# Attention and SwiGLU on one core: an earlier weight load, down weights split between copies, and bank readings moved behind a phase's last copies

## The chip, the core and the metric

The kernel runs on one core of a Trainium2 chip. Its engines work side by side, each through its own list of instructions in order: TensorE (PE, matmuls; PEld is its weight load), VectorE (DVE), ScalarE (ACT), GpSimd (POOL) and SyncE (SP), which issues most of the DMAs. The metric is the device time of one execution in microseconds (us), as the median of several runs; less is better. One execution is also profiled, and times inside it count from its first instruction.

## What is computed

```python
xn = layernorm(x)                        # x: 2048 x 512, fp32
q, k, v = heads(xn @ wqkv)               # 32 heads of 16
s = softmax(q @ k.T * 16 ** -0.5) @ v    # full attention, no mask
s = merge(s) @ wo
g = silu((silu(xn @ w_gate) * (xn @ w_up)) @ w_down)    # hidden width 1792
out = x + s * g
```

All products are made in fp32 precision: an operand is split into a rounded part (hi) and a remainder (lo), and three matmuls (hi hi, lo hi, hi lo) stand for one.

## The kernel before

**A prologue** (up to about 160 us of the span) makes layernorm, the projections q, k and v, and stores them to DRAM. It also makes the first gate and up tile of the FFN. Its last DMA is the store of the last value rows (`made()`, line 835). The buffers of the main part (`att`, lines 839 to 849: `kst`, `vst`, `hh`, `wd`) lie in memory that the prologue used.

**The main part** runs attention and the FFN as one interleaved stream. Attention has 32 units (8 groups of 4 heads by 4 query tiles of 512), each over 16 key tiles. The stream is cut into 101 **blocks** (line 464 on) of 3 to 6 key tiles, numbered from 0 in what follows. In each block, TensorE first runs a list of events, and then `values` (line 375) multiplies the block's probabilities with v into the bank `acc[0]`; `x32`, `x40` and `x48` matmuls of line 379 are the values of 4, 5 and 6 key tiles.

The events of a block come from `events` (line 483), which writes the order out by formula:

- **F**: one step of the other work (FFN, then the output projection): two matmuls that run side by side, one into each of the banks `bankx` and `banky` (`both`, line 184). `fill` (line 442) takes the next step from a generator: `ffn(b)` (line 195), then `project_out` (line 342).
- **D**: the scores of one pair of heads, straight into a PSUM buffer, from which ScalarE takes the exponential (line 889).
- **A, B**: the scores of a pair, one half each, into the one spare bank (`acc[1]`). VectorE copies each half to SBUF (lines 901 and 907), and ScalarE takes the exponential later, from the copy (line 913). B can't start until the copy of A has left the bank, and the next A waits for the copy of B.

How many pairs of a block go by A and B is `copied` (line 487): the smaller of `need` and `fit` (line 486).

**The FFN's order.** A gate and up tile (7 in a group, two groups for each of 4 token tiles) is one phase of 24 steps, then follow four down phases of 21 steps (line 234), one for each 128 tokens. One phase goes into one block. `load_gu` (line 121) loads gate and up weights for the tile after the next, 512 KB into one of two `gur` buffers, and `split_gu` splits them for the next tile; `split_wd` (line 151) splits one tile of down weights. Splits are **chores**: VectorE work in a list with a cost in step lengths. The loop of a block (line 909) puts a chore out when the VectorE has room before its next copy; `tidy` (line 139) puts out all that are left at once. `tidy` is called ahead of a block's last F (line 880), at a block's end (line 914), and in the first step of a group's first down phase (line 233), right behind `split_wd` of the group's last tile (line 230).

**Bank readings.** Behind the last step of a down phase, VectorE reads both banks (lines 241 and 242, or 245 and 246), and the output projection does the same (lines 353 and 354, or 359 and 360). They are put out in the same step as the last matmul.

**Ends.** When a unit is through, `finish` (line 407) adds chores in the unit after it: transpose `acc[0]` (line 390), a reciprocal (395), a multiplication (399), and in every second group a second transpose (415), at the end of the kernel also a split (425, 429). They go to the list at the second D.

Of the kernel before, what the change touches and what calls it, by code (L numbers as in the profile page):

```python
# [9 lines left out]
F32 = mybir.dt.float32  # L10
# [4 lines left out]
ALU = mybir.AluOpType  # L15
# [4 lines left out]
P = 128  # L20
S = 2048
D = 512
# [3 lines left out]
NB = 4  # L26
TB = S // NB
NT = TB // P
# [3 lines left out]
NF = F // P  # L32
# [18 lines left out]
def tile_block(ctx: ExitStack, tc: tile.TileContext, x, wqkv, wo, w_gate, w_up, w_down, out):  # L51
# [15 lines left out]
    one = ctx.enter_context(tc.tile_pool(name="one", bufs=1))  # L67
# [71 lines left out]
    def tidy(room=None):  # L139
        while chores and (room is None or chores[0][0] <= room):  # L140
            cost, work = chores.pop(0)
            work()  # L142
            if room is not None:
                room -= cost
# [19 lines left out]
    def catch_up():  # L164
        while after:
            after.pop(0)()
# [25 lines left out]
        pool.dma_start(g_d[r:r + P], y)  # L192


    def ffn(b):
        for grp, part in enumerate(GROUPS):
            nf = part.stop - part.start
            for f in range(nf):
                i = b * NF + part.start + f
                if i + 1 < NB * NF:  # L200
                    split_gu(i + 1)
                if f:
                    split_wd(f - 1, i - 1)
                    chores.append((0, partial(load_wd, i)))
                elif i:
                    load_wd(i)
                if i + 2 < NB * NF:
                    load_gu(i + 2)
                hi, lo = gu.pop(i)
                n = 0  # L210
                for c in range(DC):
                    for wt, j in ((hi, 0), (hi, 1), (lo, 0)):
                        both(wt[:, c], fx[:, j, c], n == 0, n == 3 * DC - 1)
                        n += 1
                        if n == 3 * DC:
                            th = one.tile([P, TB], F32, tag="th", name="th")
                            ga = two.tile([P, TB], F32, tag="ga", name="ga")
                            act(th, bankx, AF.Tanh, scale=0.5)  # L218
                            dve.scalar_tensor_tensor(ga, th, 1.0, bankx, op0=ALU.add, op1=ALU.mult)  # L219
                            dve.scalar_tensor_tensor(ga, ga, 0.5, banky, op0=ALU.mult, op1=ALU.mult)  # L220
                            kept.append((f, ga))
                            if now == 0:
                                kept.insert(0, first_hidden)
                            if now >= 0:
                                split_hidden()
                            if grp == 1 and f == nf - 1 and b + 1 < NB:
                                load_fx(b + 1, 0)
                                load_fx(b + 1, 1)
                        yield 3 * DC - n
            split_wd(nf - 1, b * NF + part.stop - 1)  # L230
            if grp == 1 and b == NB - 1:
                chores.append((0, partial(load_wo, 0)))
            tidy()
            for t in range(NT):
                n = 0
                for f in range(nf):
                    for a, w in ((0, 0), (0, 1), (1, 0)):
                        both(hh[:, f, a, t * P:(t + 1) * P], wd[:, f, w], n == 0, n == 3 * nf - 1)
                        n += 1
                        if n == 3 * nf and grp == 0:  # L240
                            dve.tensor_copy(facc[:, t], bankx)
                            dve.tensor_add(facc[:, t], banky, facc[:, t])
                        elif n == 3 * nf:
                            y = two.tile([P, D], F32, tag="ga", name="y")
                            dve.tensor_add(y, bankx, facc[:, t])
                            dve.tensor_add(y, banky, y)
                            after.append(partial(store_gate, y, b * TB + t * P))
                            if b == NB - 1:
                                after.append(partial(next_out, t))
                        yield 3 * nf - n  # L250


# [84 lines left out]
    def store_out(t, y):  # L337
        pool.tensor_mul(y, y, gt[t % NT])
        pool.tensor_add(xr[t], y, xr[t])
        (pool if t < end - 1 else sp).dma_start(out[rows[t]], xr[t])  # L340

    def project_out(b, n=DT):
        catch_up()
        for j in range(NT if n == DT else EARLY):
            t = b * NT + j
            i = 0
            for c in range(n):
                for a, w in ((0, 0), (0, 1), (1, 0)):
                    both(lhs[b, c][a][:, j * P:(j + 1) * P], fx[:, w, c], i == 0, i == 3 * n - 1)
                    i += 1  # L350
                    if i == 3 * n and n == DT:
                        y = one.tile([P, D], F32, tag="th", name="y")
                        dve.tensor_scalar(y, bankx, 0.5, None, op0=ALU.mult)
                        dve.scalar_tensor_tensor(y, banky, 0.5, y, op0=ALU.mult, op1=ALU.add)
                        store_out(t, y)
                        if b + 2 < NB:
                            after.append(partial(load_gates, t + NT))
                    elif i == 3 * n:
                        dve.tensor_copy(facc[:, j], bankx)
                        dve.tensor_add(facc[:, j], banky, facc[:, j])  # L360
                    yield 3 * n - i

    def load_gate():
# [119 lines left out]
    def events(n, f):  # L483
        length = 2 * n + f
        need = 2 * n - max(2, (10 * length + 46) // 40)
        fit = 1 if ends and length < 24 else (10 * length + 34) // 112
        copied = max(0, min(need, fit)) if now else 0
        direct = 2 * n - copied
        gap = max(4, min(5, (length - 8) / max(1, direct - 2)))
        marks = [(0, "D"), (1, "D")] + [(7 + gap * i, "D") for i in range(direct - 2)]  # L490
        marks += [(2.2 + max(5.6, min(8, (length - 5) / (2 * copied))) * i, "AB"[i % 2]) for i in range(2 * copied)]
        marks.sort(key=lambda mark: mark[0] - 0.6 * (mark[1] == "D"))
        out = []
        at = left = 0
        for t, kind in marks:
            while left < f - (kind != "D") and at < t:
                out.append((at, "F"))
                left += 1
                at += 1
            out.append((at, kind))  # L500
            at += 1 if kind == "D" else 0.5
        return direct, out + [(at + i, "F") for i in range(f - left)]
# [340 lines left out]
    wd = att.tile([P, FG, 2, D], F32R, name="wd")  # L843
    score = [spool.tile([P, 2, 512], F32, name=f"score{i}") for i in range(2)]
    spare_bank = acc[1]
    ring(2, RING, att)
    queries(1, att)
    load_k(0, 2)
# [8 lines left out]
    def run(u, first, n):  # L857
# [19 lines left out]
        final = max(at for at, (_, e) in enumerate(todo) if e == "F")  # L877
        free = 0
        for at, (t, e) in enumerate(todo):
            if at == final:  # L880
                tidy()
            if e == "F":
                fill(1)
            elif e == "D":
                kt, j = straight[done]
                for h in order():
                    scores(score[done % 2][:, h], kt, j, h)
                probs[kt, j] = ppool.tile([P, 2, TB], F32, tag="pr", name="pr")
                act(probs[kt, j], score[done % 2], AF.Exp, scale=0.25)  # L889
                done += 1  # L890
                if done == 2:
                    while ends:
                        ends.pop(0)()
                    out_steps()
            elif e == "A":
                kt, j = copies.pop(0)
                waiting.append((kt, j))
                scores(spare_bank, kt, j, 0)
                lower = True
                probs[kt, j] = ppool.tile([P, 2, TB], F32, tag="pr", name="pr")  # L900
                dve.tensor_copy(probs[kt, j][:, 0], spare_bank)  # L901
                free = copying.pop(0) + 3
            else:
                kt, j = waiting[-1]
                scores(spare_bank, kt, j, 1)
                lower = False
                dve.tensor_copy(probs[kt, j][:, 1], spare_bank)  # L907
                free = copying.pop(0) + 3
            while chores and at < final and (not copying or max(free, t) + chores[0][0] <= copying[0] + 0.5):
                free = max(free, t) + chores[0][0]  # L910
                chores.pop(0)[1]()
# [28 lines left out]
            ends.append(partial(finish, u))  # L940

    fill(total)
    catch_up()
    assert not queue and not after and given == total
    hi = two.tile([P, 2, D], F32R, tag="guh", name="rh")[:, 0]
# [75 lines left out]
```

## Time and profile before

| | us |
|---|---|
| median of 3 runs | 1419.13 (1418.51 to 1419.31) |
| the profiled execution | 1417.5 |
| its span, first to last instruction | 1415.7 |
| TensorE busy | 1399.6 (99%) |
| ScalarE busy | 1081.4 (76%) |
| VectorE busy | 756.9 (53%) |
| GpSimd busy | 92.0 (7%) |
| mean granted TensorE clock | 0.999 |

A busy TensorE is not one at its peak: matmuls are pipelined, so the time between two starts matters, not the duration of one. A row of the timeline has the start, the length, the engine, the line, the operation, its tiles and how many were merged; in square brackets stand the idle time of the engine just before it, and who ended that. A row of the chain has start, length and what ran.

### The profile page before, as it was taken

How to read it: one execution, taken by the hardware profiler on the slowest of the kernel's cores; microseconds unless marked ns; L12 is line 12 of the kernel's file. 1: busy time of each engine (PE TensorE's matmuls, PEld its weight loads, DVE VectorE, ACT ScalarE, POOL GpSimd, SP SyncE). 2: the span in 40 equal slices, each digit the busy share in tenths (PEclk: the TensorE clock that was granted, in tenths of full speed). 3: DMA queues.
4: the chain of work that ended last, by engine and by line, in shares of the span. 5: the costliest groups of instructions: out<-in, count | busy, mean ns of one | idle time of the engine just before them, and what ended most of it. 6: DMA issues, size and time to landing. Idle time of an engine off the chain costs nothing.

```text
span 1415.7 us, 27730 instructions
## 1 busy us (share of the span) xinstructions
PE 1399.6 (99%) x11227; PEld 853.3 (60%) x11227; DVE 756.9 (53%) x1281; ACT 1081.4 (76%) x1235; POOL 92.0 (7%) x104
## 2 busy tenths in 40 slices
PE   9999999999999999999999999999999999999998
PEld 7777665566555655565566556655565565565555
DVE  6543455346545653555456545654565346556566
ACT  6733587787788777887887788778877787787885
POOL 4200200000000000000000000000000000000333
PEclk9999999999999999999999999999999999999999
DMA  7768642034543421144524403256224123234332
GB/s 220 262 243 255 168 111 57 13 87 93 116 108 106 116 62 35 47 120 101 123 67 105 103 13 72 73 145 148 63 67 114 31 46 72 68 92 137 118 110 101
DMA packets 126956, 148.17 MB, mean 105 GB/s; under 512 B 12524, under 2 KB 79340, under 8 KB 126052
## 3 DMA queue, kind: packets, MB, share of 16 engines
q1 hardware_dynamic: 121620, 125.79, 34.8%
q0 software_dynamic: 4912, 20.12, 3.8%
q8 instruction: 91, 1.49, 0.5%
q14 instruction: 45, 0.37, 0.1%
q10 hardware_dynamic: 288, 0.39, 0.1%
HBM read 106.68 MB, written 39.58 MB: 103 GB/s over the span
## 4 chain that ended last, share of the span: by engine, by line
PE 86%; DVE 1%; ACT 1%; issue 0%; DVEq 0%; ACTq 0%
PE acc L379 32%; PE bankx L186 24%; PE score L873 16%; PE banky L186 11%; PE acc L873 3%; ACT pr L889 1%; PE acc L958 0%; DVE wd L142 0%; PE banky L958 0%; DVE o L390 0%; DVE pr L901 0%; PE score L958 0%; DVE o L415 0%; DVE on L399 0%; DVE rl L395 0%
## 5 line engine op out<-in xcount | busy, mean ns | idle before, releaser
L889 ACT ACTIVATE pr<-score 128x1024 f32<-128x1024 f32 x861 | 813.8, 1033 | 241.3 <-PE score L873 240.1
L379 PE MATMUL acc<-pr,vst 128*17 128x512 f32 x4096 | 463.7, 593 | 0.0
L873 PE MATMUL score<-qst,kst 50*128 50x512 f32 x1722 | 395.1, 414 | 1.7 <-ACT pr L889 1.7
L186 PE MATMUL bankx<-fx,guh 64*128 64x512 f32 x896 | 334.0, 393 | 0.1
L186 PE MATMUL banky<-fx,guh 64*128 64x512 f32 x896 | 325.4, 393 | 0.0
L379 PEld LDWEIGHTS acc<-pr,vst 128*17 128x17 f32 x4096 | 111.2, 97 | 293.2 <-issue 266.6
L873 PEld LDWEIGHTS score<-qst,kst 50*128 50x128 f32 x1722 | 174.6, 184 | 150.4 <-issue 75.7
L901 DVE COPY pr<-acc 128x512 f32<-128x512 f32 x163 | 112.7, 691 | 185.2 <-PE acc L873 180.0
L186 PE MATMUL bankx<-wd,hh 64*128 64x512 f32 x672 | 200.1, 392 | 0.0
L186 PE MATMUL banky<-wd,hh 64*128 64x512 f32 x672 | 197.4, 392 | 0.0
L186 PEld LDWEIGHTS bankx<-fx,guh 64*128 64x128 f32 x896 | 166.9, 186 | 18.8 <-issue 0.9
L186 PE MATMUL banky<-fx,gul 64*128 64x512 f32 x448 | 175.8, 392 | 0.0
L186 PE MATMUL bankx<-fx,gul 64*128 64x512 f32 x448 | 175.8, 392 | 0.0
L186 PEld LDWEIGHTS banky<-fx,guh 64*128 64x128 f32 x896 | 166.8, 186 | 6.1
L913 ACT ACTIVATE pr<-pr 128x1024 f32<-128x1024 f32 x163 | 167.7, 1080 | 0.0
L907 DVE COPY pr<-acc 128x512 f32<-128x512 f32 x163 | 112.6, 691 | 78.2 <-PE acc L873 69.0
L873 PE MATMUL acc<-qst,kst 50*128 50x512 f32 x326 | 131.5, 403 | 6.7 <-DVE pr L901 3.8
L219 DVE SCALAR_TENSOR_TENSOR ga<-th,bankx 128x512 f32<-128x512 f32 x56 | 38.5, 687 | 179.2 <-ACT th L218 179.2
L186 PEld LDWEIGHTS bankx<-wd,hh 64*128 64x128 f32 x672 | 124.9, 186 | 11.9
L186 PEld LDWEIGHTS banky<-wd,hh 64*128 64x128 f32 x672 | 124.5, 186 | 4.2
L186 PEld LDWEIGHTS bankx<-fx,gul 64*128 64x128 f32 x448 | 83.9, 187 | 11.0
L186 PEld LDWEIGHTS banky<-fx,gul 64*128 64x128 f32 x448 | 83.7, 187 | 2.8
(169 smaller groups left out, 1315.5 us busy)
## 6 DMA issues: line engine op xcount, KB each, us to landing
gur<-in_B_w_gate_dram SPq DMA_DIRECT2D x56, 256.0 KB
gur<-in_B_w_up_dram SPq DMA_DIRECT2D x56, 256.0 KB
wdr<-in_B_w_down_dram SPq DMA_DIRECT2D x56, 256.0 KB
kst<-k_d SPq DMA_DIRECT2D x192, 64.0 KB
qst<-q_d SPq DMA_DIRECT2D x192, 64.0 KB
fx<-xt_d SPq DMA_DIRECT2D x24, 512.0 KB
q_d<-parts SPq DMA_DIRECT2D x16, 512.0 KB
k_d<-parts SPq DMA_DIRECT2D x16, 512.0 KB
```

Source lines behind the costliest of these rows:

```text
L186: mm(banks[i], lhs[halves[i]], rhs[halves[i]], start=start, stop=stop)
L219: dve.scalar_tensor_tensor(ga, th, 1.0, bankx, op0=ALU.add, op1=ALU.mult)
L379: mm(acc[0][h * 32:h * 32 + DH + 1], v[:, kt % CT, h * (DH + 1):(h + 1) * (DH + 1)], probs[kt, h // 2][:, h % 2], start=kt == 0, stop=kt = ...
L873: mm(bank, k[r, j, kc * P:(kc + 1) * P], q[r, j], start=True, stop=True)
L889: act(probs[kt, j], score[done % 2], AF.Exp, scale=0.25)
L901: dve.tensor_copy(probs[kt, j][:, 0], spare_bank)
L907: dve.tensor_copy(probs[kt, j][:, 1], spare_bank)
L913: act(probs[kt, j], probs[kt, j], AF.Exp, scale=0.25)
```

## The change

There are four edits.

1. `load_gu(3)` stands ahead of `ring(2, ...)`, behind the prologue; the same load is left out at its place in tile 1 of the FFN.
2. In a group's first down phase, `tidy()` moves from the first step to the one that first uses the group's last down tile (step 19 of 21). Until then the chores of `split_wd` are put out by the block's loop.
3. The bank readings become functions in a list, `closing`. The block's loop calls them behind each event, once no A or B is left in the block. The `tidy` ahead of the block's last F is left out while an A or B is still to come.
4. `fit` becomes `(10 * length + 55) // 112` without the special case of 1 in short blocks that begin with chores of `finish`. Worked out for all 101 blocks, this changes `copied` in three of them, 88, 92 and 96, the first ones of the last three units, from 1 to 2. All other lists of events stay as they are.

```diff
+    closing = []
+    def close():
+        while closing:
+            closing.pop(0)()
+    def first_half(t):
+        dve.tensor_copy(facc[:, t], bankx)
+        dve.tensor_add(facc[:, t], banky, facc[:, t])
+    def second_half(b, t):
+        y = two.tile([P, D], F32, tag="ga", name="y")
+        dve.tensor_add(y, bankx, facc[:, t])
+        dve.tensor_add(y, banky, y)
+        after.append(partial(store_gate, y, b * TB + t * P))
...
-                if i + 2 < NB * NF:
+                if i + 2 < NB * NF and i != 1:
                     load_gu(i + 2)
...
             split_wd(nf - 1, b * NF + part.stop - 1)
             if grp == 1 and b == NB - 1:
                 chores.append((0, partial(load_wo, 0)))
-            tidy()
             for t in range(NT):
                 n = 0
                 for f in range(nf):
+                    if t == 0 and f == nf - 1:
+                        tidy()
                     for a, w in ((0, 0), (0, 1), (1, 0)):
                         both(hh[:, f, a, t * P:(t + 1) * P], wd[:, f, w], n == 0, n == 3 * nf - 1)
                         n += 1
                         if n == 3 * nf and grp == 0:
-                            dve.tensor_copy(facc[:, t], bankx)
-                            dve.tensor_add(facc[:, t], banky, facc[:, t])
+                            closing.append(partial(first_half, t))
...
+                            closing.append(partial(second_half, b, t))
...
+    def whole_out(b, t):
+        y = one.tile([P, D], F32, tag="th", name="y")
+        dve.tensor_scalar(y, bankx, 0.5, None, op0=ALU.mult)
+        dve.scalar_tensor_tensor(y, banky, 0.5, y, op0=ALU.mult, op1=ALU.add)
+        store_out(t, y)
...
                     if i == 3 * n and n == DT:
...
+                        closing.append(partial(whole_out, b, t))
                     elif i == 3 * n:
...
+                        closing.append(partial(first_half, j))
...
-        fit = 1 if ends and length < 24 else (10 * length + 34) // 112
+        fit = (10 * length + 55) // 112
...
     spare_bank = acc[1]
+    load_gu(3)
     ring(2, RING, att)
...
         for at, (t, e) in enumerate(todo):
-            if at == final:
+            if at == final and not copying:
                 tidy()
...
                 free = copying.pop(0) + 3
+            if not copying:
+                close()
             while chores and at < final and (not copying or max(free, t) + chores[0][0] <= copying[0] + 0.5):
...
     fill(total)
+    close()
     catch_up()
```

More of the change, by code (lines that the diff above doesn't have):

```diff
@@ L192, in store_gate @@
         pool.dma_start(g_d[r:r + P], y)
+    closing = []
[10 more added lines that the diff above has]
+        after.append(partial(store_gate, y, b * TB + t * P))
+        if b == NB - 1:
+            after.append(partial(next_out, t))
     def ffn(b):
@@ L240, in ffn @@
                         if n == 3 * nf and grp == 0:
-                            dve.tensor_copy(facc[:, t], bankx)
-                            dve.tensor_add(facc[:, t], banky, facc[:, t])
+                            closing.append(partial(first_half, t))
                         elif n == 3 * nf:
[L244 to L249, printed above, removed]
+                            closing.append(partial(second_half, b, t))
                         yield 3 * nf - n
@@ L340, in store_out @@
         (pool if t < end - 1 else sp).dma_start(out[rows[t]], xr[t])
+    def whole_out(b, t):
[3 more added lines that the diff above has]
+        store_out(t, y)
+        if b + 2 < NB:
+            after.append(partial(load_gates, t + NT))
     def project_out(b, n=DT):
@@ L351, in project_out @@
                     if i == 3 * n and n == DT:
[L352 to L357, printed above, removed]
+                        closing.append(partial(whole_out, b, t))
                     elif i == 3 * n:
-                        dve.tensor_copy(facc[:, j], bankx)
-                        dve.tensor_add(facc[:, j], banky, facc[:, j])
+                        closing.append(partial(first_half, j))
                     yield 3 * n - i
```

## The prediction

> **What bounds the kernel.** I read the engines' totals first, then who waited for whom on TensorE, then the chain.
>
> ```profile
> span 1415.7 us, 27730 instructions
> PE 1399.6 (99%) x11227; PEld 853.3 (60%) x11227; DVE 756.9 (53%) x1281; ACT 1081.4 (76%) x1235; POOL 92.0 (7%) x104
> ```
>
> ```profile
> PE acc L873 <- DVE pr L901: 3.8, 3, 1.5
> PE acc L873 <- issue: 2.9, 1, 2.9
> ```
>
> TensorE is the bound, so only what shortens its stream counts. Two kinds of pause stand out: three B scores (line 873 into the spare bank) that waited 3.8 us in total for the copy of line 901, and one pause of 2.9 us that the view can't name. The stream can also be slow without a pause, so the price of a pause is taken from the chain: from the start of one block's values to the start of the next's, beside a block with the same list of events.
>
> ```profile
> 171.53 0.67 PE score L873 x4
> 174.30 2.94 issue
> 185.00 5.27 PE acc L379 x48
> 198.98 5.28 PE acc L379 x48
> ```
>
> Block 1 starts at 171.53 and its values at 185.00: 13.47 us. Block 2 has the same list; it starts at 185.00 + 5.27 = 190.27 and its values at 198.98: 8.71 us. Block 1 is 4.76 us too long, of which the pause is 2.94. The windows view shows the rest; its last four numbers are granted clock, DMA share and GB/s behind the busy times:
>
> ```profile
> 174.30:177.20 2.90, 0.00 (x0) 0.00 (x0) 1.36 (x3) 0.59 (x1) 0.00 (x0) 0.97 1.07 228
> 177.20:180.40 3.20, 3.16 (x16) 2.73 (x18) 2.16 (x4) 1.19 (x2) 0.00 (x0) 0.50 0.81 186
> ```
>
> Behind the pause TensorE ran 3.2 us at half clock, 0.50 x 3.2 = 1.6 us lost; 2.94 + 1.6 = 4.5 of the 4.76.
>
> **Edit 1, the load ahead of the ring.** Why the pause? The queues of VectorE, SyncE and TensorE there:
>
> ```profile
> 175.84 0.69 DVE L911 CAST guh<-gur 128x1024 fp32r<-128x1024 f32 x1 [3.37 <-DMA gur<-in_B_w_up_dram]
> 176.45 0.68 DVE L901 COPY pr<-acc 128x512 f32<-128x512 f32 x1
> ```
>
> ```profile
> 160.64 0.39 SPq L835 DMA_DIRECT2D v_d<-vt  x1
> 166.06 3.69 SPq L98 DMA_DIRECT2D kst<-k_d  x6
> 170.97 0.63 SPq L125 DMA_DIRECT2D gur<-in_B_w_up_dram  x1
> ```
>
> ```profile
> 172.28 0.40 PE L873 MATMUL acc<-qst,kst 50*128 50x512 f32 x1
> ```
>
> The split of tile 3 stood ahead of the copy of A in VectorE's queue and waited 3.37 us for its weights, whose second half was issued at 170.97 and landed 4.87 us later. It was that late because SyncE stood at the keys of `ring(2, ...)` until 166.06, when the prologue's memory came free. In the changed kernel the load follows the store of line 835 at about 161.0; its buffer's last reader, the split of tile 1, is a chore of the prologue. With two issues of about 0.65 and 4.87 us to land it is there at about 167.2, before block 1 begins. A itself (the last row, line 873 into the spare bank) ends at 172.68. VectorE is free at 175.84 - 3.37 = 172.47: the cast ends about 173.16, the copy of A about 173.85, and TensorE reaches B at 174.30. Nothing waits by 0.4 us, so the whole 4.76 us go. The next loads (down weights, keys) move up by the two issues that leave their place, some 1.3 us.
>
> What it adds lies at 161 to 167: 512 KB beside the store of the value rows, ahead of the keys. At the 228 GB/s of the first row of the windows view it takes 2.3 us. Nothing shows which transfer gives way, so its cost to block 1 lies between 0 and 2.3 us; a gain below nothing is excluded, as the wait is priced already. I take 0: SyncE puts both into one queue, the store first, and the keys take 3.69 us to issue, longer than the 2.3.
>
> The Trainium skill ("DMA: Bandwidth & Descriptors", Queues, rings and completion order) speaks against part of this: each DMA engine takes descriptors in ring order, so the keys' data would stand behind the load's. That is the first rival below.
>
> **Edit 2, the last down weights.** The three waits for line 901 in the chain, and an undisturbed block with the same list (the last two rows):
>
> ```profile
> 239.06 4.51 PE acc L379 x40
> 252.18 4.42 PE acc L379 x40
> 664.00 4.51 PE acc L379 x40
> 677.79 4.42 PE acc L379 x40
> 703.23 4.42 PE acc L379 x40
> 715.18 4.42 PE acc L379 x40
> 1089.42 4.51 PE acc L379 x40
> 1103.25 4.42 PE acc L379 x40
> ```
>
> Values to values they take 13.12, 13.79 and 13.83 us (blocks 6, 39 and 72), against 11.95 (block 42): 1.17 + 1.84 + 1.88 = 4.89 us too many. All three are first down phases that also carry the chores of `finish`. VectorE in block 39:
>
> ```profile
> 668.54 0.72 DVE L390 STREAM_TRANSPOSE o<-acc 128x512 f32<-128x512 f32 x1 [0.63 <-PE acc L379]
> 669.29 0.25 DVE L395 RECIPROCAL rl<-o 128x16 f32<-128x16 f32 x1
> 670.67 0.38 DVE L142 CAST wd<-wdr 128x512 fp32r<-128x512 f32 x1
> 671.09 0.69 DVE L142 TENSOR_TENSOR wd<-wdr,wd 128x512 fp32r<-128x512 f32 x1
> 671.70 0.68 DVE L901 COPY pr<-acc 128x512 f32<-128x512 f32 x1
> ```
>
> `tidy` in the first step put out everything ahead of the copy of A: multiplication, second transpose, cast and remainder. Without it the loop puts out the transpose and reciprocal (3 + 1 steps, room until 5), then the copy at about 669.6, 2.1 us earlier; B was held 1.5 at most. So the waits go, and these blocks become like block 42, whose `finish` chores already lie between copies.
>
> What is late next? By the loop's own rule, block 6 puts the cast behind its first A and the remainder behind its first B; blocks 39 and 72 put the cast behind the second A and the remainder behind the second B, the last copy. In block 42 that place is here:
>
> ```profile
> 713.34 0.69 DVE L907 COPY pr<-acc 128x512 f32<-128x512 f32 x1 [0.74 <-PE acc L873]
> 714.54 0.39 PE L186 MATMUL bankx<-wd,hh 64*128 64x512 f32 x1
> ```
>
> The remainder would start at about 713.95 and end at 714.64; step 20, the first to use it, stands at 714.54. So 0.1 to 0.2 us of wait in two blocks: 0.3 in all. At the other five group ends the cast and remainder lay ahead of A without a wait in the list above, and one of them now lies behind: 0. Two DMAs move along: the store of the second transpose (line 417) and, in block 83, the load of wo (line 232) go about 1 us later; both are read only in later blocks, so 0. Sum of edit 2: 4.89 - 0.3 = 4.6.
>
> **Edits 3 and 4, the projection.** In blocks 0 to 87 no copy follows the last F, so the readings keep their place. They move in 88 to 96, where `fit` also gives one more copied pair to 88, 92 and 96.
>
> ```profile
> 1290.16 0.66 PE score L873 x4
> 1299.80 0.67 PE score L873 x4
> ```
>
> ```profile
> 1327.65 0.47 PE score L873 x2
> 1337.02 0.66 PE score L873 x4
> 1346.26 0.65 PE score L873 x4
> ```
>
> Blocks with one copied pair: 88 takes 9.64 us, 92 takes 9.37 (96 likewise). Block 93, with two: 9.24. If the three become like 93, they gain 0.40 + 0.13 + 0.13 = 0.66. The reading's move:
>
> ```profile
> 1341.82 0.69 DVE L353 TENSOR_SCALAR y<-bankx 128x512 f32<-128x512 f32 x1 [0.25 <-PE bankx L186]
> 1343.15 0.68 DVE L907 COPY pr<-acc 128x512 f32<-128x512 f32 x1
> ```
>
> ```profile
> 1337.55 5.74 ACT L889 ACTIVATE pr<-score 128x1024 f32<-128x1024 f32 x6 [1.88 <-PE score L873]
> 1343.16 2.00 ACT L913 ACTIVATE pr<-pr 128x1024 f32<-128x1024 f32 x2
> ```
>
> The last copy starts up to 1343.15 - 1341.82 = 1.3 us sooner, but ScalarE is busy without a break to 1345.16 and takes its second copied pair only at 1344.16: nothing gained, nothing lost. For the chores of `finish` that now wait until block 88's end, I bound the loss by the 0.66 itself, and take a gain of 0.4 for both edits, within -0.7 to 0.7.
>
> **Sum.** 4.76 + 4.6 + 0.4 = 9.8 us. The profiled execution took 1417.5 (1.8 around its span), which becomes 1407.7. The median, 1419.13, is 1.6 above it; the cause isn't shown, and I take it to stay: 1419.13 - 9.8 = **1409.3**.
>
> **Rivals.**
>
> *The load gets in the way* (11%). If the store lands 2.3 us later, or the keys do, A or the queue behind the store moves by up to as much and B waits again: 1409.3 + 1.8 = 1411.1, at most 1411.6. For it: a DMA share of 1.07 behind 174.30 shows that the engines can be full. Against: A had its keys at 172.28 without a wait, and they move by less than the 2.3.
>
> *The slow clock was of this execution alone* (12%). Then the median kernel loses only the pause, and edit 1 brings 4.76 - 1.6 = 3.2: 1410.9. The trace has a clock of 0.50 behind this one pause and none behind the 1.5 us waits, so a pause of 2.94 may just reach it. The Trainium skill ("TensorE: Matmul & The Clock Gate", Part 1) has the clock halve after an idle window of about 3.4 us, free-running; by that a pause of 2.94 us need not halve it, though in this trace it did.
>
> *The split ends last* (8%). If cast and remainder both came behind the last copy, 0.42 + 0.69 us from 713.95, step 19 (one step, 0.23, ahead of 714.54) would wait 0.1 and step 20 0.5: in all eight groups 8 x 0.5 = 4, so 1413.
>
> *Slower: the banks come free too late* (3%). Behind the last copy stand two readings, 0.69 each, and the next block's first F must wait for them. It decides when copy and readings, 2.1 us behind the last B, outlast the values and first scores, about 4.8 us. In block 93 the readings would end near 1344.2, and the next F stands behind the scores that start at 1346.26 and take 0.65: 2.7 us to spare. If other VectorE work went between and held F by 2 us in nine blocks: +18, 1427. Against it: nothing is put out between them.
>
> *The change doesn't do what it says* (4%): the load still waits for the prologue's memory and the copies for the splits: 1419.
>
> Forecast: 62%, its own range 1408 to 1410.6. A measurement of this kernel tells about 0.2% (2.8 us) from no change. Faster by more: 62 + 11 + 12 + 8 = 93%, of which I give one to the middle; within: 4 + 1 = 5%; slower: 3%. The range: low 1407.8 (edits 3 and 4 at their best, the 0.3 saved, and 0.9 of scatter), high 1412.5, which holds the first two rivals and half of the third.
>
> **What will show it.** The row for a wait of line 873 on `issue` gone, clock 1.00 around 177, block 1 at about 8.7 us: edit 1. No wait on line 901 above 0.3, blocks 6, 39 and 72 at about 12.0 to 12.2 values to values: edit 2. Blocks 88, 92 and 96 at about 9.25 and line 901 at 166 copies: edits 3 and 4. I am wrong if TensorE waits for `gur` or `kst` near 172, or VectorE's splits of `wd` end behind the last copy in more than two blocks.

## The result, and the profile after

The changed kernel takes 1409.41 us in the median (1409.33 to 1409.59, 4 runs), against 1418.82 before in the same comparison (1417.43 to 1419.31, 4 runs). The ratio is 0.9935, with a 95% interval of 0.9918 to 0.9953: 9.4 us faster, where 1409.3 was forecast. Its profiled execution took 1409.33, 8.2 less than the one before.

The page and TensorE's waits of the changed kernel (its lines are shifted: 889 was 873, 917 was 901, 394 was 379, 929 was 911):

```profile
span 1407.5 us, 27726 instructions
PE 1398.8 (99%) x11227; PEld 851.8 (61%) x11227; DVE 759.2 (54%) x1287; ACT 1081.7 (77%) x1235; POOL 92.8 (7%) x104
```

```profile
PE acc L889 <- DVE pr L917: 0.8, 2, 0.5
```

The pause on `issue` is gone, and so are the three waits for the copy of A. The 0.8 us of the row above are two new waits in the projection, 0.3 us in block 89 and 0.5 in block 90. TensorE is busy for 0.8 us less than before while the span is 8.2 shorter: what went was idle time and matmuls at half clock. The chain, start to start of values, for blocks 1 and 2 and then for blocks 6, 39 and 72:

```profile
168.11 3.56 PE acc L394 x32
171.67 0.67 PE score L889 x4
180.83 5.27 PE acc L394 x48
194.78 5.27 PE acc L394 x48
...
234.86 4.42 PE acc L394 x40
246.79 4.42 PE acc L394 x40
...
658.58 4.42 PE acc L394 x40
670.76 4.42 PE acc L394 x40
...
1082.29 4.42 PE acc L394 x40
1094.47 4.42 PE acc L394 x40
```

Block 1 takes 180.83 - 171.67 = 9.16 us in place of 13.47; blocks 6, 39 and 72 take 11.93, 12.18 and 12.18 in place of 13.12, 13.79 and 13.83. The granted clock (third number from the right) in the windows that held the pause and the 0.50 behind it before:

```profile
174.30:177.20 2.90, 2.78 (x24) 2.58 (x25) 2.85 (x6) 2.58 (x3) 0.00 (x0) 1.00 0.66 177
177.20:180.40 3.20, 3.20 (x30) 3.12 (x27) 1.51 (x3) 3.20 (x5) 0.00 (x0) 1.00 0.98 216
```

The projection lost time. From the values of block 87 to those of block 90:

```profile
1278.05 3.37 PE acc L394 x24
...
1306.62 4.13 PE acc L394 x32
```

That is 28.57 us; before it was 27.50 (1286.79 to 1314.29). The account of the profiled executions: block 1 -4.3, blocks 6, 39 and 72 -4.4, blocks 88 to 90 +1.07, blocks 92, 93, 96 and 97 -0.2. That makes -7.9 of the span's -8.2; 0.3 lie in small differences elsewhere.

### The profile page after: what moved, and what is told of

Same layout as the page of the kernel before. It is cut to its first block, busy times and chain, and to the rows that moved or that the text cites. A ratio compares the mean times of both kernels' runs of the same rounds, so it can differ in the third digit from the quotient of the medians.

```text
span 1407.5 us, 27726 instructions
## 1 busy us (share of the span) xinstructions
PE 1398.8 (99%) x11227; PEld 851.8 (61%) x11227; DVE 759.2 (54%) x1287; ACT 1081.7 (77%) x1235; POOL 92.8 (7%) x104
## 4 chain that ended last, share of the span: by engine, by line
PE 87%; DVE 1%; issue 0%; ACT 0%; DVEq 0%
PE acc L394 32%; PE bankx L186 23%; PE score L889 17%; PE banky L186 12%; PE acc L889 3%; PE acc L977 0%; PE banky L977 0%; DVE wd L293 0%; ACT pr L905 0%; DVE wd L294 0%; PE score L977 0%; DVE pr L917 0%; DVE pr L923 0%; DVE y L984 0%; DVE hh L444 0%
## 5 line engine op out<-in xcount | busy, mean ns | idle before, releaser
L917 DVE COPY pr<-acc 128x512 f32<-128x512 f32 x166 | 114.8, 691 | 181.3 <-PE acc L889 178.7
L923 DVE COPY pr<-acc 128x512 f32<-128x512 f32 x166 | 114.8, 692 | 78.2 <-PE acc L889 65.8
```

## The experiments

Nine kernels were run, each with a profile and at least five timed runs, against the kernel before. The table has the blocks in which the profiles differ, in us, from the first matmul of the values of the block ahead to the first of its own (block 1 has 3.56 us of values in it). The last row is the median time; the medians come from three comparisons, in which the kernel before had 1418.82 (the changed kernel), 1418.94 (the next four columns) and 1418.04 (the last three).

| block | before | changed | edit 1 | edit 2 | 3 and 4 | 88 kept | 1 and 2 | spread | last |
|---|---|---|---|---|---|---|---|---|---|
| 1 | 17.02 | 12.72 | 12.48 | 17.31 | 17.51 | 12.37 | 12.33 | 12.39 | 12.47 |
| 6 | 13.12 | 11.94 | 13.12 | 11.94 | 13.13 | 11.94 | 11.95 | 11.93 | 11.95 |
| 39 | 13.79 | 12.18 | 15.40 | 12.18 | 13.81 | 12.18 | 12.20 | 12.20 | 11.97 |
| 72 | 13.83 | 12.18 | 13.83 | 12.19 | 13.83 | 12.17 | 12.20 | 12.18 | 11.96 |
| 88 | 9.45 | 8.76 | 9.45 | 9.45 | 8.75 | 9.44 | 9.45 | 9.44 | 9.45 |
| 89 | 8.68 | 9.76 | 8.67 | 8.68 | 9.76 | 8.67 | 8.68 | 8.68 | 8.68 |
| 90 | 9.37 | 10.05 | 9.37 | 9.36 | 10.05 | 10.06 | 9.37 | 9.25 | 9.23 |
| 92 + 93 | 18.59 | 18.45 | 18.61 | 18.59 | 18.47 | 18.46 | 18.59 | 18.50 | 18.49 |
| 96 + 97 | 17.96 | 17.89 | 17.95 | 17.91 | 17.87 | 17.85 | 17.95 | 17.82 | 17.83 |
| median | 1418.82 | 1409.41 | 1412.87 | 1414.16 | 1419.34 | 1408.79 | 1408.20 | 1408.26 | 1407.70 |

### Each edit alone

**Edit 1**, the kernel before with these lines:

```diff
-                if i + 2 < NB * NF:
+                if i + 2 < NB * NF and i != 1:
...
     spare_bank = acc[1]
+    load_gu(3)
     ring(2, RING, att)
```

> Edit 1 alone, the load ahead of the ring. My theory: the pause and the slow clock behind it go, so block 1 takes 9.16 us (as in the changed kernel) in place of 13.47, and the span falls by 4.3; the three waits of 1.2 to 1.9 us in blocks 6, 39 and 72 stay. Rival, the slow clock is of single executions: the profile may gain 4.3, but the median gains 2.9 to 3.3 only. Rival, the load gets in the way: the store or the keys land up to 2.3 us later and block 1 takes over 10 us.

Measured: 1412.87 us against 1418.94, ratio 0.9959 (0.9946 to 0.9973). Block 1 falls by 4.54 us, a little more than in the changed kernel. The first rival falls: the median gains 6.1 us, not 2.9 to 3.3. So does the second: block 1 takes 12.48 - 3.56 = 8.92 us, not over 10. But block 39, which this kernel leaves alone, took 15.40 us in this profile in place of 13.79. Its waits and the window behind that block's wait (line 874 is before's 873):

```profile
PE acc L874 <- DVE pr L902: 3.8, 3, 1.5
```

```profile
668.70:672.10 3.40, 3.40 (x18) 2.78 (x16) 1.14 (x2) 2.05 (x2) 0.00 (x0) 0.50 1.07 208
```

The waits are as long as before, 3.8 us, but here the one in block 39 was followed by 3.4 us at half clock, which cost 1.6 us. A pause of 1.5 us can slow the clock too; it did in this execution and didn't in that of the kernel before.

**Edit 2**, the kernel before with these lines:

```diff
-            tidy()
             for t in range(NT):
                 n = 0
                 for f in range(nf):
+                    if t == 0 and f == nf - 1:
+                        tidy()
```

> Edit 2 alone, the group's last down weights split between the copies. My theory: blocks 6, 39 and 72 fall from 13.12, 13.79 and 13.83 us, values to values, to about 11.95, 12.2 and 12.2, 4.4 us in all; block 1 stays at 13.5. Rival, the split ends last: 12.4 or more in blocks 39 and 72 and a wait in other first down phases, so a gain of 2 to 3 us.

Measured: 1414.16 us against 1418.94, ratio 0.9965 (0.9951 to 0.9978). The three blocks fall as expected, by 1.18, 1.61 and 1.64, 4.4 in all, and no other does. The rival falls.

**Edits 3 and 4**, the changed kernel without edits 1 and 2.

> Edits 3 and 4 alone, the bank readings and the number of copied pairs. From the trace of the changed kernel I now expect a loss and not the 0.4 us gained of the forecast: from the values of block 87 to those of block 90 27.5 us before and 28.6 here, 1.1 more, and 0.2 less in blocks 92 and 96 together, so 0.9 us slower than the kernel before. Rival: the loss in blocks 88 to 90 comes from what the other edits shifted, and alone the two edits gain 0.2 to 0.7.

Measured: 1419.34 us against 1418.94, ratio 1.0006 (0.9997 to 1.0015). In the time this is unclear; by blocks it is not: 88 to 90 take 28.56 us, 1.06 more than before, just as in the changed kernel. The loss is these two edits' own.

**Edits 1 and 2**, the kernel before with both diffs above.

> Edits 1 and 2 together, without 3 and 4. Theory: the parts add up block by block, so this kernel has block 1 at 9.2 us, blocks 6, 39 and 72 at 11.9, 12.2 and 12.2, and blocks 88 to 97 as before; edits 3 and 4 cost the changed kernel 0.9 net, so this one is at 1408.5. Rival: the edits need one another, and without 3 and 4 the gain is under 8 us.

Measured: 1408.20 us against 1418.04, ratio 0.9932 (0.9918 to 0.9945). Block by block the parts add up. The medians add up less well: 6.1 and 4.8 us for each edit alone, 9.8 for both. The two edits alone are 1.2 us faster than all four, and 0.95 faster than a repeat of the changed kernel in the same comparison (1409.15, below).

### Where edits 3 and 4 lose

**Block 88 keeps one copied pair**, all else as in the changed kernel:

```diff
-        fit = (10 * length + 55) // 112
+        fit = 1 if ends and length < 20 else (10 * length + 55) // 112
```

> The changed kernel, but block 88 keeps one copied pair as before (92 and 96 keep their two). Theory: in block 88 the second copied pair pushes the chores of the unit's end behind the last copy, where VectorE piles up and holds the copies of A in blocks 89 and 90; with one pair that is gone, 87 to 90 takes 27.4 to 27.6 us again, and the kernel is 1.1 us faster than the changed one, 1408.3. Rival: the loss comes from the moved readings or from the slow casts beside GpSimd in block 89, and 87 to 90 stays at 28.3 or more.

Measured: 1408.79 us, ratio 0.9932 (0.9918 to 0.9945); 87 to 90 takes 28.17 us. Half right: block 89 is back at 8.67, while 88 gives back its 0.7, so the second copied pair cost 0.4 net. VectorE's rows from block 88's last copy to block 89's copy of A, first with two copied pairs (the changed kernel), then with one:

```profile
1286.85 0.69 DVE L923 COPY pr<-acc 128x512 f32<-128x512 f32 x1 [0.78 <-PE acc L889]
...
1292.71 0.68 DVE L917 COPY pr<-acc 128x512 f32<-128x512 f32 x1
```

```profile
1283.94 0.69 DVE L923 COPY pr<-acc 128x512 f32<-128x512 f32 x1 [0.48 <-PE acc L889]
...
1292.12 0.69 DVE L917 COPY pr<-acc 128x512 f32<-128x512 f32 x1 [2.17 <-PE acc L889]
```

The same transposes, readings and splits stand between the two copies in both. With two pairs they start about 2.8 us later in the block, and VectorE works without a gap until the copy of A; with one it idles 2.17 us there.

Block 90 stays at 10.06. Its loss has another cause, and VectorE's timeline around the end of block 89, in the changed kernel and before, shows a candidate:

```profile
1296.61 0.69 DVE L923 COPY pr<-acc 128x512 f32<-128x512 f32 x1 [0.58 <-PE acc L889]
...
1298.54 0.42 DVE L293 CAST wd<-wd 128x512 fp32r<-128x512 f32 x1
1298.99 1.70 DVE L294 TENSOR_TENSOR wd<-wd 128x512 fp32r<-128x512 f32 x1
1300.61 1.50 DVE L293 CAST wd<-wd 128x512 fp32r<-128x512 f32 x1
1302.15 0.69 DVE L294 TENSOR_TENSOR wd<-wd 128x512 fp32r<-128x512 f32 x1
1302.76 0.68 DVE L917 COPY pr<-acc 128x512 f32<-128x512 f32 x1
```

```profile
1298.86 1.28 POOL L351 TENSOR_TENSOR y<-y,gt 128x512 f32<-128x512 f32 x1 [24.65 <-ACT pr L931]
1300.22 1.61 POOL L352 TENSOR_TENSOR pair<-y,pair 128x512 f32<-128x512 f32 x1
```

```profile
1304.54 0.69 DVE L353 TENSOR_SCALAR y<-bankx 128x512 f32<-128x512 f32 x1 [0.17 <-PE bankx L186]
...
1306.47 1.29 DVE L280 CAST wd<-wd 128x512 fp32r<-128x512 f32 x1
1307.79 1.65 DVE L281 TENSOR_TENSOR wd<-wd 128x512 fp32r<-128x512 f32 x1
1309.37 0.41 DVE L280 CAST wd<-wd 128x512 fp32r<-128x512 f32 x1
```

Casts and remainders that lie beside GpSimd's two operations take 1.3 to 1.7 us in place of 0.42 and 0.69. In both kernels two of the four do, and VectorE works without a gap to block 90's copy of A (the last row of the first fence; before it starts at 1310.42). But before, the first reading started ahead of the copy of the last B, and now everything stands behind that copy. By the starts of block 89's values on TensorE, 1304.86 before and 1296.50 now, the sequence begins 0.32 us ahead of them there and 0.11 behind them here. It takes 1310.42 - 1304.54 = 5.88 us there and 6.15 here. So the copy of A comes 0.7 us later, and TensorE waits 0.5 for it. The Trainium skill ("SBUF — State Buffer", Terms) has VectorE and GpSimd share one pair of ports that the holder keeps for a whole instruction; the slow rows agree, which end at 1300.69 and 1302.11, 0.55 and 0.28 us behind the ends of GpSimd's two operations.

**The splits spread**: as above, and

```diff
-        for b, c in {early: ((0, 0), (0, 1)), early + 1: ((0, 2), (1, 0)), early + 2: ((1, 1), (1, 2)),
+        for b, c in {early: ((0, 0), (0, 1)), early + 1: ((0, 2), (1, 0)), early + 3: ((1, 1),), early + 4: ((1, 2),),
```

> As the run with block 88 kept at one copied pair, but the two splits at the end of block 89 go to the ends of blocks 90 and 91, one each. Theory: block 90 takes 10.06 us there because VectorE, after the later readings, makes two pairs of casts and remainders beside GpSimd's work, 1.50 and 1.70 us in place of 0.42 and 0.69, and the copy of A stands behind them. With the splits gone block 90 falls to 9.3 to 9.4, and the kernel to 1408.1. Rival: it is the number of copies that fills these blocks, and block 90 stays at 10.0 or the loss moves to 91 and 92.

Measured: 1408.26 us, ratio 0.9934 (0.9920 to 0.9947). Block 90 falls to 9.25, and 91 and 92 don't rise. VectorE now idles ahead of block 90's copy of A:

```profile
1297.49 0.69 DVE L358 SCALAR_TENSOR_TENSOR y<-banky,y 128x512 f32<-128x512 f32 x1
1301.49 0.69 DVE L917 COPY pr<-acc 128x512 f32<-128x512 f32 x1 [3.31 <-PE acc L889]
```

With the splits gone and the readings where edit 3 puts them the loss is gone; without edit 3 and with the splits (edits 1 and 2 alone) it is gone too. It takes both. How much of the 0.68 us is GpSimd's slowing and how much the work of the two splits is not shown, as this run takes both out of the way. In the median this run can't be told from edits 1 and 2 alone.

### The last 0.25 us of blocks 39 and 72

```diff
             split_wd(nf - 1, b * NF + part.stop - 1)
+            for k in [k for k, (_, work) in enumerate(chores) if getattr(work, "__name__", "") == "turn_out"]:
+                chores.append(chores.pop(k))
```

> As the run with the spread splits, and in a group's first down phase the second transpose of a unit's end goes behind the split of the last down weights. Theory: in blocks 39 and 72 the remainder then lies ahead of the second A and not behind the last copy, so the 0.25 us that these blocks have over 11.93 go, 0.5 in all: 1407.6. Rival: the 0.25 has another cause, and blocks 39 and 72 stay at 12.18.

Measured: 1407.70 us (1407.48 to 1407.91), ratio 0.9926 (0.9913 to 0.9940). Blocks 39 and 72 fall to 11.97 and 11.96. All five runs lie below all runs of the changed kernel, and below all of its repeat in the same comparison (1408.97 to 1409.88). In the chain and on VectorE, the remainder of the last down weights (line 931 here) now comes early in block 39:

```profile
658.25 4.42 PE acc L396 x40
670.22 4.42 PE acc L396 x40
```

```profile
665.90 0.68 DVE L931 TENSOR_TENSOR wd<-wdr,wd 128x512 fp32r<-128x512 f32 x1
```

### What the early load needs, and what made the pause

**The load behind `ring(2, ...)`**, else as in the changed kernel:

```diff
-    load_gu(3)
     ring(2, RING, att)
     queries(1, att)
+    load_gu(3)
     load_k(0, 2)
```

> The changed kernel with the load behind ring(2, ...) and ahead of the keys. It can then be issued from 166.8 on only, when SyncE is let go, and pushes the keys back by its own issue, 1.3 us. Theory: its data lands 4.9 us after its second issue, near 172.9, just when VectorE comes to the cast, so block 1 takes at most 1 us more than 9.16, and the median is within 1 us of the changed kernel. Rival, the keys are late: A waits, block 1 takes over 10.5 us and the kernel 1411 or more. Rival: the early issue doesn't matter and nothing changes.

Measured: 1409.15 us, ratio 0.9937 (0.9924 to 0.9951); block 1 takes 12.50 us, as in edit 1 alone. The experiment did not do what I wrote. SyncE was let go at once:

```profile
161.51 1.63 SPq L125 DMA_DIRECT2D gur<-in_B_w_gate_dram  x1
163.20 1.29 SPq L125 DMA_DIRECT2D gur<-in_B_w_up_dram  x1
166.75 3.81 SPq L98 DMA_DIRECT2D kst<-k_d  x6
```

It is the keys' own DMAs that wait for the memory, and `ring` puts nothing on SyncE. So this run is a repeat of the changed kernel: it shows that the load need only stand ahead of the keys, and nothing about how late it could be.

**The cast behind the copy**, the kernel before with the load left late:

```diff
-        chores.append((3, partial(dve.tensor_copy, hi, raw)))
+        chores.append((5 if i == 3 else 3, partial(dve.tensor_copy, hi, raw)))
```

> The kernel before, with the load where it was, but the cast of tile 3 gets a cost of 5 in place of 3, so that the block's loop puts it behind the copy of A and not ahead of it. Theory: it is VectorE's order that turns the late weights into the pause; then A's copy runs at 172.7 and B at 174.3 without a wait, the copy of B stands behind the cast instead, and the second A waits about 1 us for it. So the pause falls from 2.94 to about 1, no slow clock follows it, block 1 takes about 10 us in place of 13.47, and the kernel gains 2.5 to 4.5 us. Rival: TensorE waits in block 1 for something else that lands late (keys, the weights themselves), and block 1 stays above 12 us.

Measured: 1414.98 us against 1418.78, ratio 0.9973 (0.9962 to 0.9984). VectorE's rows, TensorE's wait and the window:

```profile
175.29 0.69 DVE L901 COPY pr<-acc 128x512 f32<-128x512 f32 x1 [0.21 <-PE acc L873]
178.94 0.69 DVE L911 CAST guh<-gur 128x1024 fp32r<-128x1024 f32 x1 [2.96 <-DMA gur<-in_B_w_up_dram]
179.55 0.68 DVE L907 COPY pr<-acc 128x512 f32<-128x512 f32 x1
```

```profile
PE acc L873 <- DVE pr L907: 1.8, 1, 1.8
```

```profile
177.00:180.40 3.40, 1.64 (x16) 1.00 (x13) 1.46 (x3) 2.30 (x3) 0.00 (x0) 1.00 1.04 216
```

The copy of A runs without a wait for the weights, the cast still waits 2.96 us, and the pause moves to the second A and shrinks to 1.8 us; I had expected 1. No slow clock follows. Block 1 takes 14.27 - 3.56 = 10.71 us, 2.75 less than before, with the weights as late as ever. So TensorE never waited for the weights themselves: VectorE's order turned them into the pause.

## Why the prediction was right, point by point

**Edit 1** (4.76 forecast, 4.3 measured). The cause and the cure were as written, which edit 1 alone and the cast behind the copy both show. The size was 0.45 us too large, though nothing waited for the weights. In the changed kernel the load's two issues took 2.00 and 1.02 us in place of about 0.65 each, and the keys were let go 6.04 us after the store was issued, in place of 5.42:

```profile
161.27 2.00 SPq L125 DMA_DIRECT2D gur<-in_B_w_gate_dram  x1
163.32 1.02 SPq L125 DMA_DIRECT2D gur<-in_B_w_up_dram  x1
166.80 3.69 SPq L98 DMA_DIRECT2D kst<-k_d  x6
```

Whether the load did that isn't clear: from the store's issue to the keys it is 5.66 to 6.04 us in the seven profiles with the early load, and 5.42 to 5.76 in the four without. Nor is it what pushed VectorE's queue, which had 0.70 us of idle time to give. The rows before and after:

```profile
168.77 0.69 DVE L219 SCALAR_TENSOR_TENSOR ga<-th,bankx 128x512 f32<-128x512 f32 x1 [0.70 <-ACT th L218]
170.16 0.42 DVE L142 CAST hh<-ga 128x512 fp32r<-128x512 f32 x1
```

```profile
168.89 0.69 DVE L237 SCALAR_TENSOR_TENSOR ga<-th,bankx 128x512 f32<-128x512 f32 x1
170.29 0.97 DVE L142 CAST hh<-ga 128x512 fp32r<-128x512 f32 x1
173.06 0.80 DVE L929 CAST guh<-gur 128x1024 fp32r<-128x1024 f32 x1
173.78 0.67 DVE L917 COPY pr<-acc 128x512 f32<-128x512 f32 x1
```

The queue is only 0.1 us late until the cast of `hh`, which took 0.97 us in place of 0.42. The prediction let VectorE's rows keep their lengths. GpSimd's clearing of `kst` (line 89) starts when the store has landed and ran from 166.85 to 173.31 beside that cast; that this slowed it fits the other slow casts, but was not tested by itself. So the cast of tile 3 starts at 173.06 and not at 172.47, and the copy of A ends at 174.45 where 173.85 was forecast: the 0.4 us to spare were gone, and TensorE started B at 174.56, 0.52 us behind the step before it, where such steps start about 0.23 apart. In the seven profiles with edit 1 the cast of `hh` takes 0.57 to 0.97 us and block 1 12.33 to 12.72 in the table's count, in nearly the same order, and the changed kernel has the longest of both.

**Edit 2** (4.6 forecast, 4.4 measured). Right in each term. The late remainder was foreseen with 0.1 to 0.2 us for each of two blocks and cost 0.25:

```profile
668.68 0.69 DVE L923 COPY pr<-acc 128x512 f32<-128x512 f32 x1 [0.41 <-PE acc L889]
669.29 0.68 DVE L929 TENSOR_TENSOR wd<-wdr,wd 128x512 fp32r<-128x512 f32 x1
```

It ends at 669.97, and step 20 starts behind it. The run in the table's last column took this wait away by order alone.

**Edits 3 and 4** (0.4 gained forecast, within -0.7 to 0.7; 0.9 lost). This step failed, and by a little more than its bounds. It looked at one block at a time: that ScalarE gains nothing from an earlier copy in block 93 was right, that 88, 92 and 96 come down was right as well (8.76, 9.22 and 9.28 us, from 9.45, 9.93 and 9.96). It didn't follow VectorE's queue into the next block. In block 88 the second copied pair put the last copy about 2.8 us later, with the chores of the unit's end and the readings still behind it, and delayed block 89 by 1.08 us; in block 89 the moved readings started VectorE's full queue later, with two splits in it that GpSimd slows, and block 90 lost 0.68. The prediction had bounded the loss by those chores by 0.66 us, the gain of the copied pairs, without a row for it. The copied pairs also only shift work between neighbours: 92 gains 0.70 and 93 gives back 0.56.

**The sum.** On the profiled execution 9.8 were forecast and 8.2 came. The median still met the forecast because a second assumption failed the other way, that the 1.6 us between the median and the profiled execution before would stay. They went; the changed kernel's profiled run is within 0.1 of its median. That the two misses cancel is luck: the mechanisms of edits 1 and 2 were right, the closeness of the median was not earned.

What the 1.6 us were stays open. One candidate is slow clock that the profiled execution had less of. Of the 24 runs of the kernel before that were timed beside edits 1 and 2, alone or together, the two fastest, 1415.79 and 1416.01, had a mean granted clock of 0.999, and the ten with a clock of 0.997 took 1418.71 to 1420.05. A difference of 0.002 is 2.8 us of 1416, about what parts them (one run at 0.999 took 1418.07, and a clock is given to 0.001 only, so it isn't all of the scatter). The lower clock goes with block 1's pause: the five runs of edit 1 alone lie at 0.999, four of the five of edit 2 alone at 0.997 or 0.998, the changed kernel at 0.999 and 1.000. But no profile here shows more than one slow stretch up to the last values (that of the cast behind the copy has its one in the prologue).

The other candidate is the prologue. Block 0's values start at 167.90 us in the kernel before and at 167.94 to 168.31 in the seven profiles with edit 1, but at 168.62, 169.39 and 170.49 in the other three (edits 3 and 4, edit 2 alone, the cast behind the copy), and in these a matmul of the prologue (line 660 in the kernel before) waits 1.4 to 1.8 us for ScalarE, in place of 0.7 to 0.9. The profile of edits 3 and 4 needs no second slow stretch to lie at its median: its span is 1.9 us above that of the kernel before, 0.7 by the prologue, 0.5 by a longer pause in block 1 (3.31 us), and the rest about what the two edits cost. The rival that the slow clock was of the profiled execution alone falls either way, as each of the three profiles with block 1's pause has it.

## What to carry to other kernels

Price a pause by block against an undisturbed block with the same list of work, not by the wait in the profile: clock and queue come with it. When work on an in-order engine is put off, follow its queue through the next block or two, and see who shares its ports there. Where an engine's order, and not the missing data, makes the wait, moving one chore behind another brings much of what an earlier load does: 2.75 us of block 1 here, against 4.54. A median that lands on the forecast proves little as long as the terms haven't been checked one by one.

## What the runs showed of the hardware

A stretch of about 3.4 us at half clock can go with a TensorE pause that is shorter than the stretch. All three profiles that have block 1's pause (2.94 us in the kernel before, 3.17 in edit 2 alone, 3.31 in edits 3 and 4) show one. Of the eight pauses of 1.5 us in the four profiles without edit 2, one was followed by it (block 39, edit 1 alone), and the pause of 1.8 us (the cast behind the copy) wasn't. Each costs about 1.6 us. Its start isn't tied to the pause: it began at 177.0 in the kernel before, 0.2 us ahead of the pause's end, and at 179.9 in edits 3 and 4, 1.5 us behind it. The Trainium skill ("TensorE: Matmul & The Clock Gate", Part 1) speaks of at least one idle window of about 3.4 us, free-running; the length of the slow stretch agrees, while here a partly idle window was enough, as no pause was 3.4 us long. Which of the short pauses meets it looks like chance; that was not tested by itself.
